# Raw query weights loaded second on SP's queue instead of on ScalarE's, with three dummy matmuls fewer in the ramp

## The chip, the cores and the metric

The kernel runs on one core of a Trainium2 chip. The metric is the device time of one launch in microseconds (us), lower is better. The time before is the median of three runs, 265.23 us (265.18 to 267.19). One more execution is recorded by the hardware profiler; all views of the profile come from that one.

## The reference

One sequence of 2048 tokens of width 448 goes through two blocks with adaptive layer norm. Scale, shift and gate of each come from one conditioning vector `c`. Block A is linear attention with 16 heads of width 28; its features are the softmax of a small product with `w_phi` and the softmax of the negated product. Block B is a gated MLP whose gate mixes tokens with a 2048 x 2048 matrix.

```python
mod = (_silu(c) @ w_mod).reshape(c.shape[0], 6, 1, -1)      # sa, ca, ga, sb, cb, gb
h = _layernorm(x) * (1 + ca) + sa
x = x + ga * A(h, wqkv, w_phi, wo)
#   A: q, k, v = split(h @ wqkv); pq = q @ w_phi; pk = k @ w_phi   (per head)
#      phi_q = [softmax(pq), softmax(-pq)]; phi_k alike
#      o = phi_q @ (phi_k^T v) / (phi_q . sum(phi_k) + 1e-6);  o @ wo
h = _layernorm(x) * (1 + cb) + sb
x = x + gb * B(h, w_in, w_sp, b_sp, w_out)
#   B: z = gelu(h @ w_in); z1, z2 = halves; g = w_sp @ layernorm(z2) + b_sp;  (z1 * g) @ w_out
```

All inputs and the output are in bf16.

## The kernel before, in words

The path that runs is `fast_path`. The tokens are 16 tiles of 128; the width of 448 is cut into four chunks of 112. The kernel is written as many small steps (functions of one or two letters). The text `ORDER` (line 482 on) lists every step with its arguments, and the program emits them in that order, so the order on each engine is this list filtered by engine, written out by hand. In a word such as `FTq:0@B1` the part after the colon is the step's argument and `@B1` is the PSUM slot; in `ld:wk/Y` the letter after the slash is the engine: Y is SP (SyncE), S ScalarE, V VectorE, G GpSimd. Engines wait for one another through semaphores that the framework sets. A DMA's semaphore is one of eight, taken in the order of the loads in the list over all queues; a load that takes a semaphore again waits for the transfer that had it before.

Before the main work the projections are prepared from the raw weights; this is the ramp, the first 17 us:

- `ld:x0` (line 641), `ld:c` (640), `ld:wq` and `ld:wk` (both through `load_rows`, line 630), `ld:phi` (634), `ld:x1`, `ld:x2` (642, 643), `ld:wsa`, `ld:wca` (637), `ld:wv` (630) and further loads are DMAs from HBM. Before, `ld:c` and `ld:wq` are issued by ScalarE, all the other loads of the ramp by SP.
- `du:n` (line 712) issues n matmuls of a zero tile into a PSUM bank that nobody reads; these are the dummies. `du:14@A2` stands directly ahead of the first transposes of the query weights.
- `ct` and `ce:1` to `ce:4` (723 to 736) form silu(c).
- `FTq:h` and `FTk:h` (line 795) transpose half of the raw query or key weights on TensorE, 8 transposes each. `ETq` and `ETk` (799 on ScalarE, 801 on VectorE) copy the results out of PSUM.
- `bd` (739) spreads `phi` into a block-diagonal tile `BD`; `PFq:m` and `PFk:m` (811) multiply the transposed weights with it, 4 products of 112 columns each; `EPq` and `EPk` (799, 801) copy the folded weights out.
- `l1s`, `l1e`, `l1r`, `l1a` (818 to 829) are the layer norm of a tile of x; `X:i` (842) turns a tile of it on TensorE, and `XE:i` (799) copies it out to `hT`.
- `csA` and `ccA` (747) form the shift and scale columns from `wsa` and `wca`; `SHq`, `SHk`, `SHv` (761) and `SC...` (770, 774) put them into the weights.

After the ramp come the products of query, key and value (`qM`, `kM`, `vM`: lines 907, 852, 860), the attention, the second block and the output. Later tiles of the layer norm are turned by DMA transposes on SP's queue (`T1`, line 834).

These few lines show how a load and the dummies are emitted:

```python
def load_rows(eng, dst, src):
    eng.dma_start(out=dst, in_=src.rearrange("(k p) n -> p k n", p=CB))
"wq": lambda q: load_rows(q, wq_raw[0:CB], A_wqkv[:, 0:D]),
def du(n, slot):
    wps = bank(slot, "warm_ps")
    for _ in range(n):
        nc.tensor.matmul(wps[:, 0, 0:256], lhsT=zero[:, 0:P], rhs=zero[:, 0:256], start=True, stop=True)
```

Of the kernel before, what the change touches and what calls it, by code (L numbers as in the profile page):

```python
# [479 lines left out]


ORDER = """
m3 m4 m1/G m2b/V m2a/V ld:x0/Y l1s:0 ld:c/S ld:wq/S du:3@A2 ct@B0 tbl ce:1 ce:2 l1e:0,1/G l1r:0,1 l1a:0/G ce:3 ce:4 du:14@A2 FTq:0@B1 du:1@A2 FTq:1@B0
ETq:0/S X:0@A2 XE:0/S ld:wk/Y FTk:1@A1 ETk:1/S FTk:0@B1 ETk:0/S ld:phi/Y ETq:1/V bd/V scb ld:x1/Y l1s:1 l1e:1,2/G l1r:1,2 l1a:1/G PFq:3@B0 PFq:2@A2
PFq:1@A1 EPq:2/S EPq:1/S ld:x2/Y EPq:3/V l1s:2 l1s:3 l1e:2,4/G l1r:2,4 du:4@A0 PFk:0@B0 PFk:2@B1 PFq:0@A2 PFk:1@A0 ld:wsa/Y du:1@A1 csA@A1 EPk:0/S
EPk:1/S PFk:3@B0 X:1@A0 EPk:3/S XE:1/S EPk:2/S EPq:0/V esA SHq@A2 ld:wca/Y ccA@B0 l1a:3/V X:3@A1 l1a:2/V ecA SCq:0/V SCq:3/V SCq:2/V SCq:1/V X:2@A0
# [692 lines left out]
```

## Time and profile before

| | |
|---|---|
| median of 3 runs | 265.23 us (265.18 to 267.19) |
| the profiled execution: its time, its span | 265.23 us, 263.3 us |
| TensorE matmuls busy | 253.3 us, 96% of the span |
| VectorE, ScalarE, GpSimd busy | 157.6, 107.7, 89.6 us |
| DMA queues q1 (SP's) and q10 (ScalarE's) | 24.05 MB and 0.82 MB |

The span runs from the first to the last instruction; times in the views are counted from its start. PE is TensorE's matmuls, PEld its weight loads, DVE is VectorE, ACT ScalarE, POOL GpSimd; SPq and ACTq are the instruction queues of SyncE and ScalarE that issue DMAs. A timeline row gives the start and the duration of a group of instructions, the operation with its output and inputs, a count, and in square brackets the idle time of the engine ahead of it and what ended it. Instructions on TensorE overlap: a duration runs to the end of the last one in the group, so the spacing of the starts is shorter than the duration of one. In a row of windows stand the stretch, its length, the busy time and count for PE, PEld, DVE, ACT and POOL, the granted clock, the busy share of the DMA engines and their GB/s. The chain of waits is followed back from the last instruction to what released each step.

### The profile page before, as it was taken

The page shows a single profiled execution, that of the slowest core. Times are in us where ns is not written, and L with a number is a line of the kernel's source. Part 1 is how long each engine was busy: PE and PEld are TensorE (multiplying, and loading weights), DVE is VectorE, ACT ScalarE, POOL GpSimd, SP SyncE. Part 2 cuts the span into 40 slices and gives each one's busy share as a digit, 9 for nine tenths or more (in the row PEclk, how much of TensorE's full clock was granted, in tenths as well). Part 3 has the DMA queues.
Part 4 walks back from the last instruction along what each step waited for, and adds up shares of the span by engine and source line. Part 5 has one row for each costly group of instructions (what it writes and reads, how often), then busy time and mean ns, then how long its engine had stood idle before and what let it go on. Part 6 is the DMA issues. An engine that isn't in the chain of part 4 may idle for free.

```text
span 263.3 us, 4375 instructions
## 1 busy us (share of the span) xinstructions
PE 253.3 (96%) x1648; PEld 137.1 (52%) x1648; DVE 157.6 (60%) x367; ACT 107.7 (41%) x222; POOL 89.6 (34%) x149
## 2 busy tenths in 40 slices
PE   6999999999799999999999999999999999999992
PEld 4864565675464554544444444444444444565691
DVE  4689999868799999785106223522371183415761
ACT  2789887646788888987720300100000000000000
POOL 6217986996388888573300000000000000000000
PEclk9999999999999999999999999999999999999999
DMA  7993987993356557869900000002009800030011
GB/s 173 277 294 69 245 149 153 213 288 76 60 96 121 107 107 133 167 131 174 169 0 4 0 0 0 20 2 75 0 2 142 157 0 2 17 105 2 0 37 61
DMA packets 68655, 25.23 MB, mean 96 GB/s; under 512 B 58129, under 2 KB 68498, under 8 KB 68626
## 3 DMA queue, kind: packets, MB, share of 16 engines
q1 hardware_dynamic: 67696, 24.05, 43.8%
q10 hardware_dynamic: 930, 0.82, 1.2%
q8 instruction: 15, 0.25, 0.4%
q14 instruction: 14, 0.11, 0.1%
HBM read 8.87 MB, written 1.84 MB: 41 GB/s over the span
## 4 chain that ended last, share of the span: by engine, by line
PE 90%; DVE 4%; DMA 2%; ACT 1%; issue 1%; POOL 1%; ACTq 0%
PE g_ps L1060 37%; PE z_ps L1044 9%; PE z_ps L1016 9%; PE o_ps L1073 8%; PE q_ps L907 5%; PE v_ps L860 4%; PE k_ps L852 4%; PE x_ps L972 3%; PE kvacc L883 3%; DMA f_wq_raw<-in_A_wqkv_dram 2%; PE num L935 2%; DVE f_t L956 2%; PE tps L795 1%; PE sh_ps L761 1%; PE sh_ps L766 1%
## 5 line engine op out<-in xcount | busy, mean ns | idle before, releaser
L1060 PEld LDWEIGHTS <-f_z2n 128*128 128x128 bf16 x560 | 50.1, 98 | 47.0
L1066 DVE TENSOR_TENSOR f_gb<-g_ps,f_bsp 128x512 f32<-128x512 f32 (+2 forms) x35 | 20.4, 583 | 55.5 <-PE g_ps L1060 55.3
L1060 PE MATMUL g_ps<-f_Eq,f_z2n 128*128 128x512 bf16 x224 | 49.5, 379 | 0.0
L1047 ACT ACTIVATE f_z1T<-z_ps 128x512 bf16<-128x512 f32 x28 | 15.6, 592 | 61.8 <-PE z_ps L1044 61.7
L1016 PE MATMUL z_ps<-f_win,f_hT 112*128 112x448 bf16 (+1 forms) x128 | 26.2, 352 | 0.0
L1044 PE MATMUL z_ps<-f_hT,f_win 113*128 113x512 bf16 (+1 forms) x112 | 26.1, 379 | 0.0
L1060 PE MATMUL g_ps<-f_hT,f_z2n 128*128 128x384 bf16 (+1 forms) x224 | 25.1, 272 | 0.0
L1060 PE MATMUL g_ps<-f_wsp,f_z2n 128*128 128x512 bf16 x112 | 24.7, 379 | 0.0
L1073 PE MATMUL o_ps<-f_wout,f_z1T 128*128 128x448 bf16 x112 | 23.0, 352 | 0.0
L1076 DVE TENSOR_TENSOR f_xpad<-o_ps,f_x 128x448 bf16<-128x448 f32 x16 | 9.6, 620 | 20.7 <-PE o_ps L1073 20.7
L1067 DVE TENSOR_TENSOR f_z1T<-f_gb,f_z1T 128x512 bf16<-128x512 f32 (+2 forms) x35 | 20.5, 585 | 1.8 <-DVE f_gb L1066 0.5
L1016 PEld LDWEIGHTS <-f_hT 112*128 112x128 bf16 (+1 forms) x128 | 12.2, 97 | 12.4 <-DMA f_hT<-f_xpad 0.8
L912 ACT ACTIVATE f_Eq<-q_ps 112x1024 bf16<-112x1024 f32 x16 | 16.1, 1030 | 5.7 <-PE q_ps L907 5.6
L1044 PEld LDWEIGHTS <-f_win 113*128 113x128 bf16 (+1 forms) x112 | 10.9, 97 | 13.0
L855 ACT ACTIVATE f_E<-k_ps 128x448 bf16<-128x448 f32 x32 | 15.9, 550 | 4.1 <-PE k_ps L852 2.5
L866 DVE TENSOR_REDUCE f_ksum<-f_E 128x32 f32<-128x896 bf16 x16 | 16.7, 1060 | 0.7 <-ACT f_E L855 0.7
L956 DVE TENSOR_TENSOR f_t<-num,f_w 128x896 bf16<-128x896 f32 x16 | 16.8, 1084 | 0.0
L1020 ACT ACTIVATE f_z2g<-z_ps 128x896 bf16<-128x896 f32 x16 | 14.7, 916 | 4.0 <-PE z_ps L1016 3.9
L1073 PEld LDWEIGHTS <-f_z1T 128*128 128x128 bf16 x112 | 10.9, 98 | 10.1
L907 PE MATMUL q_ps<-f_hT,f_Wq 113*128 113x512 bf16 (+1 forms) x64 | 15.0, 378 | 0.0
L860 PE MATMUL v_ps<-f_wv,f_hT 113*128 113x448 bf16 (+1 forms) x64 | 14.6, 352 | 0.0
L852 PE MATMUL k_ps<-f_Wk,f_hT 113*128 113x448 bf16 (+1 forms) x64 | 14.5, 352 | 0.0
(165 smaller groups left out, 347.3 us busy)
## 6 DMA issues: line engine op xcount, KB each, us to landing
out_dram<-f_xpad SPq DMA_DIRECT2D x16, 112.0 KB, 1.8
f_win<-in_B_w_in_dram SPq DMA_DIRECT2D x2, 784.0 KB, 5.7
f_x<-in_A_x_dram SPq DMA_DIRECT2D x3, 448.0 KB, 8.6
f_wm<-in_w_mod_dram SPq DMA_DIRECT2D x3, 406.0 KB, 5.7
f_wmg<-in_w_mod_dram SPq DMA_DIRECT2D x2, 392.0 KB, 9.5
f_wout<-in_B_w_out_dram SPq DMA_DIRECT2D x1, 784.0 KB, 6.9
f_bsp<-in_B_b_sp_dram SPq DMA_DIRECT2D x1, 512.0 KB, 4.5
f_wm<-in_w_mod_dram ACTq DMA_DIRECT2D x1, 406.0 KB, 5.0
```

Source lines behind the costliest of these rows:

```text
L852: nc.tensor.matmul(t[:, 0, 0:D], lhsT=hT[0:KR[m], i, m, :], rhs=Wk[0:KR[m], m, :], start=(m == 0), stop=(m == KC - 1))
L860: nc.tensor.matmul(t[:, 0, 0:D], lhsT=hT[0:KR[m], i, m, :], rhs=wv[0:KR[m], m, :], start=(m == 0), stop=(m == KC - 1))
L866: nc.vector.tensor_reduce(out=ksum[:, i], in_=Er[i % NR][:].rearrange("p s (c f h) -> p (s c) h f", c=4, h=HP), axis=AX.X, op=ALU.add)
L907: nc.tensor.matmul(t[:, u, :], lhsT=Wq[0:KR[m], m, cc * CB:cc * CB + P], rhs=hT[0:KR[m], 4 * st:4 * st + 4, m, :], start=(m == 0), stop=(m ...
L912: nc.scalar.activation(out=Eq[st // 2][0:CB, 2 * c2:2 * c2 + 2, s, (st % 2) * 512:(st % 2 + 1) * 512], in_=ps["q" + str(n)][0:CB, :, :], f ...
L956: nc.vector.tensor_tensor(out=tr[i % 2][:], in0=numv(i)[:, :, :, 0:DH], in1=wr[i // 2 % 2][:, i % 2].unsqueeze(3).to_broadcast([P, 2, H, D ...
L1016: nc.tensor.matmul(t[:, hf, 0:D], lhsT=hT[0:KR[m], i, m, :], rhs=win_s[0:KR[m], m, FH + hf * D:FH + (hf + 1) * D], start=(m == 0), stop=(m ...
L1044: nc.tensor.matmul(t[:, 0, :], lhsT=win_s[0:KR[m], m, fc * P:(fc + 1) * P], rhs=hT[0:KR[m], 4 * st:4 * st + 4, m, :], start=(m == 0), stop ...
L1060: nc.tensor.matmul(g[:, 0, 0:b - a], lhsT=later["z2n"][:, s_, fc * P:(fc + 1) * P], rhs=wspT[t][:, s_, a:b], start=(s_ == 0), stop=(s_ == ...
L1066: nc.vector.tensor_tensor(out=gb, in0=ps["G%d_%d" % (ch, fc)][:, 0, 0:b - a], in1=bsp[:, t * TCHF + a:t * TCHF + b], op=ALU.add)
L1067: nc.vector.tensor_tensor(out=z, in0=gb, in1=z, op=ALU.mult)
L1073: nc.tensor.matmul(ps["o" + str(t)][:, 0, 0:D], lhsT=later["z1T"][:, fc, t * P:(t + 1) * P], rhs=wout_s[:, fc, :], start=(fc == 0), stop=( ...
```

## The change

`ld:wq` keeps its place in the list but goes from ScalarE's queue (`/S`) to SP's (`/Y`), where it comes directly after `ld:x0` and ahead of `ld:wk`. `du:14` becomes `du:11`. On SP's queue every later load and transpose stands one place further back; on ScalarE's queue the load of `c` is directly followed by the table load. TensorE has three weight loads and three matmuls fewer. Nothing else is changed: the semaphores that the loads take are the same, as the order of the list is.

```diff
 ORDER = """
-m3 m4 m1/G m2b/V m2a/V ld:x0/Y l1s:0 ld:c/S ld:wq/S du:3@A2 ct@B0 tbl ce:1 ce:2 l1e:0,1/G l1r:0,1 l1a:0/G ce:3 ce:4 du:14@A2 FTq:0@B1 du:1@A2 FTq:1@B0
+m3 m4 m1/G m2b/V m2a/V ld:x0/Y l1s:0 ld:c/S ld:wq/Y du:3@A2 ct@B0 tbl ce:1 ce:2 l1e:0,1/G l1r:0,1 l1a:0/G ce:3 ce:4 du:11@A2 FTq:0@B1 du:1@A2 FTq:1@B0
 ETq:0/S X:0@A2 XE:0/S ld:wk/Y FTk:1@A1 ETk:1/S FTk:0@B1 ETk:0/S ld:phi/Y ETq:1/V bd/V scb ld:x1/Y l1s:1 l1e:1,2/G l1r:1,2 l1a:1/G PFq:3@B0 PFq:2@A2
 PFq:1@A1 EPq:2/S EPq:1/S ld:x2/Y EPq:3/V l1s:2 l1s:3 l1e:2,4/G l1r:2,4 du:4@A0 PFk:0@B0 PFk:2@B1 PFq:0@A2 PFk:1@A0 ld:wsa/Y du:1@A1 csA@A1 EPk:0/S
 EPk:1/S PFk:3@B0 X:1@A0 EPk:3/S XE:1/S EPk:2/S EPq:0/V esA SHq@A2 ld:wca/Y ccA@B0 l1a:3/V X:3@A1 l1a:2/V ecA SCq:0/V SCq:3/V SCq:2/V SCq:1/V X:2@A0
```

## The prediction

> **What bounds the kernel now.** I read the page's totals first, then the chain of waits for the first 20 us, then the timelines of TensorE, SP's queue and ScalarE there, and last the waits further on.
>
> ```profile
> span 263.3 us, 4375 instructions
> PE 253.3 (96%) x1648; PEld 137.1 (52%) x1648; DVE 157.6 (60%) x367; ACT 107.7 (41%) x222; POOL 89.6 (34%) x149
> PE 90%; DVE 4%; DMA 2%; ACT 1%; issue 1%; POOL 1%; ACTq 0%
> ```
>
> TensorE is busy for 96% of the span and is 90% of the chain that ends last. DMA is 2% of that chain, and the chain's first 20 us show that this is the load of the raw query weights, 5.47 of 263.3 us (start, duration, what):
>
> ```profile
> 0.72 0.54 ACTq L640
> ...
> 1.29 5.47 DMA f_wq_raw<-in_A_wqkv_dram
> ...
> 6.80 0.99 PE tps L795 x8
> ...
> 8.01 0.75 PE tps L795 x8
> ...
> 9.97 0.92 ACT f_wTk L799
> ```
>
> Up to 6.76 us the end of the kernel hangs on that one transfer: ScalarE's queue issues it second, at 1.29, and it lands 5.47 us later. TensorE's timeline shows what surrounds it:
>
> ```profile
> 2.51 3.17 PE L712 MATMUL warm_ps<-f_zero 128*128 128x256 bf16 x14
> 6.80 0.99 PE L795 MATMUL tps<-f_ident,f_wq_raw 112*112 112x112 bf16 x8 [1.13 <-DMA f_wq_raw<-in_A_wqkv_dram]
> 7.59 0.42 PE L712 MATMUL warm_ps<-f_zero 128*128 128x256 bf16 x1
> 8.98 1.45 PE L795 MATMUL tps<-f_ident,f_wk_raw 112*112 112x112 bf16 x16
> 11.13 0.60 PE L712 MATMUL warm_ps<-f_zero 128*128 128x256 bf16 x4
> 12.40 0.37 PE L811 MATMUL pf_ps<-f_BD,f_wTk 112*112 112x112 bf16 x4
> ...
> 16.91 1.90 PE L907 MATMUL q_ps<-f_hT,f_Wq 113*128 113x512 bf16 x8
> ```
>
> The fourteen dummies end at 5.68; then TensorE idles 1.13 us. A dummy comes every (3.17 - 0.42) / 13 = 0.21 us in the first row and about every 0.11 us at 11.13 (0.60 us for four, with an end of some 0.27): TensorE runs at half speed at first. (The column of the granted clock below says 1.00 even there; the spacing is the better witness.) The tile view of the key weights puts the change of speed inside their sixteen transposes, between 9 and 10 us (min/median/max in ns):
>
> ```profile
> L795 PE MATMUL tps<-f_ident,f_wk_raw x16: 215/300/301, 9.0 to 10.2; 112*112 112x112 bf16 x16
> ```
>
> So the fast clock came some 3.1 us after unbroken work began at 6.80, and it had not come by the end of the 3.17 us of dummies.
>
> **The change, part by part.** SP's queue and the landings (KB are 1024 bytes; the last column is us from issue to landing):
>
> ```profile
> 0.72 0.39 SPq L641 DMA_DIRECT2D f_x<-in_A_x_dram  x1
> 1.18 0.41 SPq L630 DMA_DIRECT2D f_wk_raw<-in_A_wqkv_dram  x1
> 1.64 0.48 SPq L634 DMA_DIRECT2D f_phi<-in_A_w_phi_dram  x1
> ...
> 6.78 0.39 SPq L644 DMA_DIRECT2D f_x<-in_A_x_dram  x1
> ```
> ```profile
> f_wk_raw<-in_A_wqkv_dram SPq DMA_DIRECT2D x1, 392.0 KB, 4.9
> f_wq_raw<-in_A_wqkv_dram ACTq DMA_DIRECT2D x1, 392.0 KB, 5.5
> f_phi<-in_A_w_phi_dram SPq DMA_DIRECT2D x1, 24.5 KB, 5.4
> ```
>
> *The load.* Its issue goes to 1.18, the present place of the key weights: 0.11 us earlier. What counts is what it shares the engines with. Now the two weights are in flight together and land at 6.76 (query) and 6.08 (key). In one queue the query weights come first and the key weights wait behind them. The traffic of these microseconds prices that (window, the busy columns, PEclk, DMA share, GB/s):
>
> ```profile
> 1.50:2.50 1.00, 1.00 (x7) 0.51 (x5) 0.93 (x5) 0.83 (x1) 1.00 (x7) 1.00 0.65 141
> 2.50:3.50 1.00, 1.00 (x6) 0.73 (x6) 0.96 (x6) 0.72 (x3) 0.31 (x1) 1.00 0.68 164
> 3.50:4.50 1.00, 1.00 (x7) 0.70 (x5) 0.71 (x5) 0.00 (x0) 0.46 (x3) 1.00 1.09 345
> 4.50:5.50 1.00, 1.00 (x6) 0.51 (x4) 0.00 (x0) 0.00 (x0) 0.89 (x3) 1.00 1.14 254
> 5.50:6.50 1.00, 0.18 (x1) 0.00 (x0) 0.00 (x0) 0.00 (x0) 0.94 (x2) 1.00 1.23 212
> 12.90:22.40 9.50, 9.47 (x88) 5.59 (x88) 8.29 (x26) 8.84 (x17) 2.59 (x6) 1.00 0.91 237
> ```
>
> x0 is 115 kB (128 x 448 x 2), each weight 401 kB. Moved in sum: 141 kB by 2.5, 305 by 3.5, 650 by 4.5, 904 by 5.5. Both weights, x0, c and phi (943 kB) are through at about 5.68; the query weights landed at 6.76, 1.1 us later. x0 plus the query weights are 516 kB, which this traffic reaches at 3.5 + 211/345 = 4.11; with the same 1.1 us the landing is **5.2**. The bounds: not before 4.84, where the shortened dummies end (below), and not after 6.08, where the key weights landed from this very place with a rival beside them. I take 5.2, as the first full-rate window (345) belongs to this stretch. That one queue can fill the engines is seen in the last row: from 12.90 on, with all loads on SP's queue, they are 91% busy.
>
> *What is behind it on SP.* All later issues slip by one issue, 0.41 us. The key weights: the same bytes ahead, so by 5.57 + 1.1 = 6.7; their first transposes stood at 8.98, or 6.9 to 7.2 after the shift, and ScalarE can't take their result before 7.9 (below), so 0.5 us is to spare. phi lands at 7.0 now and, with the same bytes ahead, then too; its user on VectorE (next row) would start at about 7.6. SP's issue at 6.78 waits for the query weights' landing (it reuses their semaphore) and comes earlier, not later; the engines are full anyway. All this is costed at nothing; without the cover each would cost its lateness, a few tenths.
>
> ```profile
> 9.34 0.61 DVE L739 TENSOR_TENSOR f_BD<-f_phi,f_bmask 112x448 bf16<-112x448 bf16 x1
> ```
>
> *ScalarE* loses one issue of 0.35 us before its table load; it is idle afterwards for 4.61 us (first row below), so nothing comes of it.
>
> *The dummies.* Eleven end at 2.51 + 11 x 0.2115 = 4.84 instead of fourteen at 5.47 (issue). They stand in front of the transposes in TensorE's order: with fourteen, a landing at 5.2 would be used only at 5.47, so this edit is worth 0.27 us of the sum.
>
> *The start of the transposes* therefore moves from 6.80 to about 5.2: **-1.6 us** (ends -0.7 and -1.96). What is late next? ScalarE's timeline:
>
> ```profile
> 7.84 0.91 ACT L799 COPY f_wTq<-tps 112x896 bf16<-112x896 bf16 x1 [4.61 <-PE tps L795]
> 9.22 0.59 ACT L799 COPY f_hT<-xt_ps 128x512 bf16<-128x512 bf16 x1 [0.48 <-PE xt_ps L842]
> 9.97 1.71 ACT L799 COPY f_wTk<-tps 112x896 bf16<-112x896 bf16 x2 [0.16 <-PE tps L795]
> 11.57 0.98 ACT L799 CAST f_Wq<-pf_ps 112x448 bf16<-112x448 f32 x2
> 13.76 0.53 ACT L799 CAST f_Wk<-pf_ps 112x448 bf16<-112x448 f32 x1 [0.34 <-PE pf_ps L811]
> ```
>
> From 7.84 on it is almost full, and waits 0.48 + 0.16 = 0.64 us for slow transposes. This is where the clock enters. The idle stretch shrinks from 1.13 us to about 0.4, so TensorE's work is nearly unbroken from 2.51 on; if 3.1 to 3.2 us of that bring the fast clock, it comes between 5.7 and, counted from the landing, 8.4, instead of near 9.9. A transpose then costs some 52 ns instead of 94: 0.75 us for eight in the chain's row at 8.01 against (0.37 - 0.215) / 3 for the fast products of the same width at 12.40. The two waits go. I estimate **-0.5 us** of the possible 0.64; the ends are 0 and, with the 0.34 at 13.76 too, -0.98. VectorE, which has no such waits before 13.5 but for its first, sets a limit of about 2 on the whole shift. Its normalised tiles (first row, done at 14.82) feed the transposes of the chain's row at 15.09, with 0.3 us of slack:
>
> ```profile
> 14.12 0.70 DVE L829 TENSOR_SCALAR f_xpad<-f_x,f_nm,f_rs 128x448 bf16<-128x448 bf16 x2 [0.43 <-POOL f_rs L826]
> ```
> ```profile
> 15.09 0.47 PE xt_ps L842 x8
> ```
>
> Here a rule of the Trainium skill ("TensorE: Matmul & The Clock Gate", Part 1) bears: the clock doubles after one busy window of about 3.4 us, and the windows run freely, so work of one window's length may straddle two. The trace agrees so far: 3.17 us of dummies didn't suffice. By the rule alone the term is the full 0.64 at a good phase, and 0 at a bad one.
>
> *From there to the end* TensorE is the bound and the shift is carried: 9.47 of 9.50 us busy from 12.90 to 22.40, and between 17 and 80 us its own waits are
>
> ```profile
> PE num L940 <- DVE f_t L956: 1.8, 1, 1.8
> PE kvacc L883 <- POOL f_phik L873: 0.4, 1, 0.4
> ```
>
> both on engines whose work descends from the same ramp and so moves with it. The sum is -1.6 - 0.5 = **-2.1 us**. The profiled execution took 265.23 us, its span 263.3 and 1.9 around it; that is also the median shown, so I forecast **263.1 us**.
>
> **The rivals.** *Earlier start, same clock* (-1.1 to -1.6): the fast clock comes near 9.9 again, and the twelve or so 112-wide products that ran fast after 9.9 run slow, at 42 ns more each 0.5 us, partly hidden. For it speaks that 3.17 us of dummies failed; against it that the gap shrinks. About 263.9.
>
> *The transfer hardly arrives earlier.* The window 2.50 to 3.50 moved only 164 GB/s; if that is the price of one queue starting, the query weights land as the key weights do, at 6.08: -0.7, 264.5. The Trainium skill ("DMA: Bandwidth & Descriptors", Issuing engines are not separate DMA queues) goes further: the issuing engine changes only issue time, as all queues share the engines. Read so, only the 0.11 us of issue is won, 265.1. Against it stands that the order of the bytes, not their rate, is changed.
>
> *Slower: the clock is lost.* If the landing stays near 6.1 while the dummies end at 4.84, the gap is 1.25 us instead of 1.13; should that delay the fast clock by another 3.2 us, to 13, then 32 products (42 ns each, 1.3 us), five dummies (0.1 each, 0.5) and 16 column products are slow, some 2.0 us less 0.5 of waits that hide it: +1.5 - 0.7 = +0.8, 266.0. It decides only from a landing past about 6.0.
>
> *More than forecast:* start at 4.84 and all of the 0.98: -2.9, 262.3.
>
> **How the numbers follow.** Forecast 0.60 (262.6 to 263.6); same clock 0.16; late landing 0.10; clock lost, or anything slower, 0.06; more 0.08. The prediction is the likeliest case's. The range 262.4 to 264.5 takes it, the same clock and most of the late landing. About 1% (2.65 us) is what a measurement here can tell from no change: below 262.6 lie the last case and the edge of the first, 0.12; above 267.9 next to nothing, 0.03; between, 0.85.
>
> **What would show it.** The query weights landing near 5.2 with about 4 us from issue; transposes of them starting there with an idle of under 0.5 us before; durations of 215 ns already in the key weights' first transposes; ScalarE's 0.48 and 0.16 gone; the first query product, at 16.91 now, near 14.8. A landing past 5.8, 300 ns throughout the key weights, or a wait of theirs on their DMA, would make it wrong; so would a first query product that is early while the span is not shorter.

## The result, and the profile after

| | before | changed |
|---|---|---|
| median of 20 runs each | 265.27 us (263.49 to 267.35) | 263.84 us (262.72 to 266.19) |
| ratio of the means of these runs, with its 95% interval | | 0.9936 (0.991 to 0.9963) |
| the profiled execution: time, span | 265.23 us, 263.3 us | 263.9 us, 262.0 us |
| means of all runs, later ones included (116 and 32) | 265.23 us | 264.13 us |
| ratio of these means, with its 95% interval | | 0.9959 (0.9944 to 0.9974) |

The change saves 1.4 us by the medians and 1.7 by the means of the first 20 runs each, and 1.1 us (0.7 to 1.5) by the means of all. Single runs of either kernel lie up to 4 us apart, and the comparison of 20 with 20 runs isn't sharp: the kernel before, compared with itself, came out at 0.9961 (0.9922 to 0.9999) of itself. The means over all runs rest on the most of them, and why the runs differ so much turned out to be part of the answer. One run of the kernel with the key weights first (268.53 us) is over 1.5% above its fastest and is left out below, and one like it of the kernel before (267.59 us) moves no difference by more than 0.03 us.

TensorE's timeline of the changed kernel, the rows that answer to those shown before:

```profile
2.49 2.53 PE L712 MATMUL warm_ps<-f_zero 128*128 128x256 bf16 x11
4.89 1.00 PE L795 MATMUL tps<-f_ident,f_wq_raw 112*112 112x112 bf16 x8
5.67 0.42 PE L712 MATMUL warm_ps<-f_zero 128*128 128x256 bf16 x1
...
7.06 1.30 PE L795 MATMUL tps<-f_ident,f_wk_raw 112*112 112x112 bf16 x16
...
9.14 0.60 PE L712 MATMUL warm_ps<-f_zero 128*128 128x256 bf16 x4
...
14.93 1.90 PE L907 MATMUL q_ps<-f_hT,f_Wq 113*128 113x512 bf16 x8
```

The idle 1.13 us ahead of the first transposes is gone, they start at 4.89 instead of 6.80, and the first query product at 14.93 instead of 16.91. SP's queue and the landings:

```profile
1.17 0.42 SPq L630 DMA_DIRECT2D f_wq_raw<-in_A_wqkv_dram  x1
1.64 0.48 SPq L630 DMA_DIRECT2D f_wk_raw<-in_A_wqkv_dram  x1
2.17 0.49 SPq L634 DMA_DIRECT2D f_phi<-in_A_w_phi_dram  x1
...
5.42 0.58 SPq L644 DMA_DIRECT2D f_x<-in_A_x_dram  x1
```
```profile
f_wq_raw<-in_A_wqkv_dram SPq DMA_DIRECT2D x1, 392.0 KB, 3.7
f_wk_raw<-in_A_wqkv_dram SPq DMA_DIRECT2D x1, 392.0 KB, 4.6
...
f_phi<-in_A_w_phi_dram SPq DMA_DIRECT2D x1, 24.5 KB, 4.3
```

The query weights land 3.7 us after their issue instead of 5.5, at 4.84; the key weights at 6.26 and phi at 6.5, both ahead of their users. Of the traffic up to this landing (GB/s in the last column) only the stretch from 2.5 to 3.5 us changed much, from 164 to 218; the next has 342 where it had 345:

```profile
2.50:3.50 1.00, 1.00 (x6) 0.72 (x6) 0.95 (x6) 0.34 (x3) 0.31 (x1) 1.00 0.77 218
3.50:4.50 1.00, 1.00 (x7) 0.72 (x5) 0.71 (x5) 0.00 (x0) 0.47 (x3) 1.00 1.09 342
```

ScalarE still waits 0.48 us for the transposes of x; the 0.16 further on is gone:

```profile
5.92 0.91 ACT L799 COPY f_wTq<-tps 112x896 bf16<-112x896 bf16 x1 [3.07 <-PE tps L795]
7.30 0.59 ACT L799 COPY f_hT<-xt_ps 128x512 bf16<-128x512 bf16 x1 [0.48 <-PE xt_ps L842]
7.99 1.71 ACT L799 COPY f_wTk<-tps 112x896 bf16<-112x896 bf16 x2
11.78 0.53 ACT L799 CAST f_Wk<-pf_ps 112x448 bf16<-112x448 f32 x1 [0.34 <-PE pf_ps L811]
```

Set side by side, instruction by instruction, TensorE in the profile of the changed kernel is 1.92 us early at the first transposes, 1.98 at the first query product, 1.85 from 40 us on, and 1.46 from 114 us on. The last 0.4 us went to a wait that the kernel before did not have in its profile, for a DMA transpose (waits of TensorE):

```profile
PE z_ps L1016 <- DMA f_hT<-f_xpad: 0.3, 1, 0.3
```

In a second profile of the same kernel (below) this wait is 0.2 us, and 2.0 us are carried to the end.

### The profile page after: what moved, and what is told of

Same layout as the page of the kernel before. It is cut to its first block, busy times and chain, and to the rows that moved or that the text cites. A ratio compares the mean times of both kernels' runs of the same rounds, so it can differ in the third digit from the quotient of the medians.

```text
span 262.0 us, 4360 instructions
## 1 busy us (share of the span) xinstructions
PE 252.3 (96%) x1636; PEld 136.5 (52%) x1645; DVE 157.7 (60%) x367; ACT 107.7 (41%) x222; POOL 89.5 (34%) x149
## 4 chain that ended last, share of the span: by engine, by line
PE 90%; DVE 4%; DMA 1%; issue 1%; ACT 1%; POOL 1%; SPq 0%
PE g_ps L1060 37%; PE z_ps L1044 9%; PE o_ps L1073 8%; PE z_ps L1016 8%; PE q_ps L907 5%; PE v_ps L860 4%; PE k_ps L852 4%; PE x_ps L972 3%; PE kvacc L883 3%; PE num L935 2%; DVE f_t L956 2%; PE warm_ps L712 2%; DMA f_hT<-f_xpad 1%; PE tps L795 1%; PE sh_ps L761 1%
```

## The experiments

Three theories stood against each other for where the gain is from. (The recorded expectations letter their own theories anew each time.) A: the order of the bytes; the query weights' bytes now come ahead of the key weights', and that start is carried to the end. B: the queue itself, SP's being quicker than ScalarE's. C: the clock, that is, how unbroken TensorE's work is while it waits. Differences of means stand with 95% intervals; the mean of the kernel before is 265.23 (116 runs), that of the changed kernel 264.13 (32). "Clock" is the mean granted clock of a run. The trace also records when the fast clock was granted; ahead of the first record the column of a view reads 1.00, so that it doesn't show the half speed at the start. The edits show only those words of `ORDER` that differ.

**The kernel before, again.** No edit.

> The kernel before once more, for its spread and the granted clock of each run. The twenty runs of the changed kernel lie in two groups: clock 0.997 to 0.999 with 262.7 to 263.9 us, and 0.990 to 0.993 with 264.25 to 266.2. Theory A: the groups come from the fast clock being lost for one stretch later in the kernel in some runs, and have nothing to do with the change: then the kernel before shows the same two groups, some 1.5 to 2 us apart, in about the same shares (the lower clock in 3 to 6 of 10), and the median of its 0.997 to 0.999 runs is about 1.5 to 2 above that of the changed kernel's, 264.9 to 265.3. Theory B: the change caused the lower group: then the kernel before has no clocks under 0.997.

Twelve runs: seven with a clock of 0.998 to 1.000 (263.5 to 264.9 us), five with 0.990 to 0.992 (264.85 to 266.55). Where each run's clock is known, 49 of 96 runs of the kernel before have a clock of 0.993 or less, with a mean of 266.10 against 264.13; of the changed kernel 12 of 32, 264.96 against 263.64. So the two groups are not of the change's making. But the expectation missed the distance of the upper groups: the changed kernel's is 0.49 us faster (0.12 to 0.82), not 1.5 to 2; in the lower groups it is 1.14 (0.67 to 1.57). The windows of this run's profile show what the lower group is:

```profile
63.80:67.10 3.30, 1.52 (x9) 0.69 (x8) 3.08 (x7) 2.91 (x6) 0.98 (x1) 1.00 0.44 89
67.20:70.50 3.30, 3.30 (x30) 2.41 (x29) 1.25 (x6) 0.94 (x4) 0.95 (x1) 0.50 0.37 70
70.70:74.00 3.30, 3.30 (x29) 1.97 (x28) 2.78 (x4) 2.87 (x6) 2.07 (x5) 1.00 0.03 5
```

In the first stretch TensorE is busy for 1.52 of 3.30 us; in the next the clock granted is 0.50. The idle time is one wait, in front of the nine dummies of `dm:9,3`:

```profile
64.39 0.92 PE L766 MATMUL sh_ps<-f_win,f_Gb 112*128 112x448 bf16 x4
67.09 0.40 PE L940 MATMUL num<-f_zero 128*128 128x32 bf16 x9 [1.78 <-DVE f_t L956]
67.33 1.76 PE L935 MATMUL num<-f_KVbd,f_Eq 112*128 112x120 bf16 x16
```

After it, sixteen products take 1.76 us; at full clock they take 1.00. The records of all traces lie on a grid of 3.413 us (in this one the clock came at 5.73, went at 67.17 and was back at 70.59), and where the grid stands to the start of the kernel differs from run to run. That is the phase, and it decides whether the 1.78 us fall into one stretch of the grid (clock lost in five of the six profiles of this study that have all of the wait, or all but 0.02 us, in one stretch) or are cut in two (kept, in the two profiles shown first). An estimate: a phase that is equally likely everywhere would put 1.78 us whole into one stretch of 3.41 in (3.41 - 1.78) / 3.41 = 48% of the runs, and 49 of 96 is 51%.

**The load alone.** Changed kernel with fourteen dummies:

```diff
-ce:3 ce:4 du:11@A2 FTq:0@B1
+ce:3 ce:4 du:14@A2 FTq:0@B1
```

> The load goes to SP's queue, the fourteen dummies stay. Theory A (the order of the bytes decides, and the dummies stand in the way): the query weights land at 4.9 as in the changed kernel, but the transposes start behind the dummies, at 5.5 instead of 4.89; the first query product at about 15.5 (14.93 in the changed kernel, 16.91 before); time 0.6 us above the changed kernel, ratio to before 0.995 to 0.997. Theory B (the dummies hide behind the landing): start at 4.9 and the same time as the changed kernel.

Landing at 5.08, start behind the dummies at 5.46, as theory A of the expectation has it. But the first query product came at 14.53, earlier than in any profile of the changed kernel, and the mean of twelve runs is 263.82: 0.31 us below the changed kernel (-0.88 to +0.24), not 0.6 above it. The tile view of the query weights tells why; the median transpose is a fast one (min/median/max in ns):

```profile
L795 PE MATMUL tps<-f_ident,f_wq_raw x16: 213/215/301, 5.5 to 6.5; 112*112 112x112 bf16 x16
```

The clock came at 5.87, right after a stretch of the grid (2.46 to 5.87) filled by dummies. ScalarE's 0.48 us of waiting is gone there:

```profile
6.26 0.91 ACT L799 COPY f_wTq<-tps 112x896 bf16<-112x896 bf16 x1 [3.41 <-PE tps L795]
7.07 0.59 ACT L799 COPY f_hT<-xt_ps 128x512 bf16<-128x512 bf16 x1
7.54 1.73 ACT L799 COPY f_wTk<-tps 112x896 bf16<-112x896 bf16 x2
```

**The dummies alone.** The load back on ScalarE's queue, eleven dummies:

```diff
-ld:c/S ld:wq/Y
+ld:c/S ld:wq/S
```

> Eleven dummies, the load stays on ScalarE's queue. Theory A: the load lands at 6.76 as before, the idle time ahead of the transposes grows from 1.13 to about 1.75 us, the first query product stays at 16.9 if the fast clock comes in the same way: ratio 1.000. Theory B (the dummies are what the gain is made of): start earlier than 6.8, ratio 0.995. Theory C (a longer idle stretch costs the fast clock): the fast clock comes later than 3.4 us after the first transpose, the first query product at 17.5 or later, ratio above 1.002.

Landing at 6.76, idle 1.79 us, clock at 11.25, first query product at 17.04. Mean 265.70: 0.47 above the kernel before (-0.23 to +1.14). Theory B of the expectation, that the gain is made of the dummies, is out; whether the longer idle time costs anything can't be told from this (eight of the twelve runs have a clock of 0.993 or less, more than the half of before).

**The key weights first.** Both on SP's queue, in the other order:

```diff
-ld:c/S ld:wq/Y du:3@A2
+ld:c/S ld:wk/Y ld:wq/Y du:3@A2
-XE:0/S ld:wk/Y FTk:1@A1
+XE:0/S FTk:1@A1
```

> Both weights on SP's queue, the key weights ahead of the query weights, eleven dummies. Theory A (the gain is that the query weights' bytes are no longer interleaved with another load's and come first): now the key weights land at about 4.9 and the query weights at about 6.2, where the key weights land in the changed kernel; the transposes start at 6.2 to 6.8, the first query product at 16.3 to 16.9, ratio 0.998 to 1.000. Theory B (SP's queue is faster than ScalarE's, whatever the order): query weights land by 5.4 and most of the gain stays, ratio 0.994 to 0.996.

```profile
f_wk_raw<-in_A_wqkv_dram SPq DMA_DIRECT2D x1, 392.0 KB, 4.1
f_wq_raw<-in_A_wqkv_dram SPq DMA_DIRECT2D x1, 392.0 KB, 4.9
```

The key weights land at 5.3, the query weights, on the same queue, at 6.58. The place in the queue decides, not the queue: theory A. The mean of eleven runs, 265.98, is even 0.78 above the kernel before (+0.15 to +1.40); beside the 35 runs of before in the same comparison the ratio is 1.0031 (0.999 to 1.0071). With eleven dummies and a late landing TensorE idles 1.71 us, and in the profile the clock, granted at 4.69, was taken away from 8.10 to 11.51. That this is the 0.78 us isn't shown: the first query product of this profile came at 16.41, and the profiles of before have 15.63 to 16.91.

**Both on ScalarE's queue.** Query, then key weights behind c; SP's queue goes on with phi and x:

```diff
-ld:c/S ld:wq/Y du:3@A2
+ld:c/S ld:wq/S ld:wk/S du:3@A2
-XE:0/S ld:wk/Y FTk:1@A1
+XE:0/S FTk:1@A1
```

> Query and key weights both on ScalarE's queue, in this order, behind c; SP's queue goes on with phi, x1 and so on right after x0. Eleven dummies. Theory A (what counts is that no other queue has bytes in flight beside the query weights): x0, phi, x1, x2 and the modulation weights share the engines with them, and they land at 5.6 to 6.5; the first query product at 15.7 to 16.6; mean 0.7 to 1.3 above the changed kernel's. Theory B (only the order of the two weights counts): they land by 5.2 and the mean is that of the changed kernel, 264.0.

```profile
f_wq_raw<-in_A_wqkv_dram ACTq DMA_DIRECT2D x1, 392.0 KB, 4.5
f_wk_raw<-in_A_wqkv_dram ACTq DMA_DIRECT2D x1, 392.0 KB, 6.3
```

Landing at 5.80, between the 4.84 to 5.55 of the kernels with the load second on SP's queue and the 6.7 of before: being first in one queue helps only as far as the other queue has little in flight. Theory A by the landing; it is one profile, and how much SP's queue had in flight was not varied further. The first query product came at 16.0. The mean, 265.88, missed the expectation: it is 1.75 above the changed kernel, not 0.7 to 1.3, and 0.66 above before (+0.10 to +1.20) although the weights land earlier. Eight of the twelve runs have a clock of 0.993 or less; what the rest of the difference is made of isn't shown.

**Few dummies.** Changed kernel with four:

```diff
-ce:3 ce:4 du:11@A2 FTq:0@B1
+ce:3 ce:4 du:4@A2 FTq:0@B1
```

> The changed kernel with four dummies instead of eleven ahead of the first transposes: TensorE idles from 3.4 to 4.9 us. Theory A (the landing sets the start, the dummies only keep the work unbroken for the clock): start at 4.9 as in the changed kernel; the fast clock comes one stretch of 3.4 us later in about half of the phases, so the first query product at 14.9 to 16.0 and the mean 0.3 to 0.8 us above the changed kernel's. Theory B (the dummies ahead do nothing): the same mean as the changed kernel's 264.0.

```profile
5.60 0.62 PE L795 MATMUL tps<-f_ident,f_wq_raw 112*112 112x112 bf16 x4 [2.08 <-DMA f_wq_raw<-in_A_wqkv_dram]
```

Here the landing was at 5.55, the clock came at 10.82, and the first query product at 16.18. The mean of 265.49 is 1.36 above the changed kernel (+0.83 to +1.88): the whole gain is lost. The dummies ahead of the landing are worth as much as the load's new place, which fits theory C and is more than either the prediction or this expectation had. That the clock carries the whole of it rests on this one profile.

**The changed kernel, again.** No edit.

> The changed kernel once more, beside the same runs of the kernel before, for the size of the difference: the query weights land near 4.9, the transposes start at 4.9, mean 263.7 to 264.3, ratio of the means to the kernel before 0.993 to 0.997. If the first comparison was luck of the phases, the ratio is 0.998 or more.

Mean of twelve 264.39; ratio of this comparison 0.9974 (0.994 to 1.0009), a little beyond the upper end of what was expected. Its profile has the phase of the first profile of before (3.18 against 3.16), and there the change shows in full: landing at 5.44 (4.9 expected), start at 5.49, clock at 6.59 (9.99 before), first query product at 14.90, TensorE 2.0 us early at its end. All transposes of the key weights are fast, and ScalarE no longer waits its 0.48 and 0.16 us:

```profile
L795 PE MATMUL tps<-f_ident,f_wk_raw x16: 213/215/215, 7.2 to 8.0; 112*112 112x112 bf16 x16
```
```profile
7.38 0.58 ACT L799 COPY f_hT<-xt_ps 128x512 bf16<-128x512 bf16 x1
7.86 1.72 ACT L799 COPY f_wTk<-tps 112x896 bf16<-112x896 bf16 x2
```

So the start is 1.32 us earlier in this pair of profiles and the first query product 2.01: here the clock gives 0.69 us.

**Without `dm:9,3`.** The dummies that stand in front of products 4 and 5 near 66 us, and wait for VectorE, are taken out of the changed kernel:

```diff
-SHw:1@B1 dm:9,3 nM:4@A1
+SHw:1@B1 nM:4@A1
```

> The changed kernel without the nine dummies of dm:9,3, which wait for VectorE near 66 us and hold up the products behind them. Theory A (the lower group of the granted clock, 0.990 to 0.993, comes from this idle stretch of 1.78 us: where one of the clock's stretches of 3.41 us holds all of it, the next one runs at half speed): without them the idle stretch is some 0.4 us, all runs have clocks of 0.997 or more, the upper half of the times (264.25 to 266.2 in the changed kernel) is gone, and the products start about 1 us earlier: 261.5 to 263.2. Theory B (the clock is lost elsewhere): the two groups stay, only shifted.

> The changed kernel without dm:9,3 once more beside the three others of this call: mean 261.8 to 262.6, clocks 0.997 or more in nearly all runs, no run above 263.5.

Six runs with a mean of 262.18 and eight with 262.10, 2.00 us below the changed kernel (-2.44 to -1.56). The wait of 1.78 us becomes one of 0.41 for ScalarE (the second of these profiles):

```profile
64.46 0.92 PE L766 MATMUL sh_ps<-f_win,f_Gb 112*128 112x448 bf16 x4
65.79 1.00 PE L935 MATMUL num<-f_KVbd,f_Eq 112*128 112x120 bf16 x16 [0.41 <-ACT f_Eq L912]
```

No run of the fourteen has a clock of 0.993 or less, where 12 of 32 had; in neither profile is the clock lost near 66 us. Four runs lie under the expected 0.997, at 0.995 and 0.996. One of them is profiled, and there the clock falls only at 258.19, when TensorE's last product has ended at 255.99. So theory A holds for the place, and the lower group of the clock is gone, as is the direct wait of some 1.4 us.

**The same for the other three kernels**, so that the change can be seen without this loss: the kernel before, the load alone, and the kernel before with nineteen dummies (`du:19` in place of `du:14`), all without `dm:9,3`.

> The kernel before without dm:9,3, so that the clock loss near 66 us no longer hides the size of the change. Theory A (the change is worth what its earlier start gives, some 1.1 to 1.7 us on average over the phases): mean 263.2 to 263.9, against 262.2 for the changed kernel without dm:9,3. Theory B (the change is worth something only through where the clock is lost later): mean 262.0 to 262.6.

> The load on SP's queue, fourteen dummies, no dm:9,3. Theory A (the three dummies are in the way of a landing at 4.8 to 5.5): start at 5.5, mean 0.2 to 0.5 above the changed kernel without dm:9,3. Theory C (what the dummies cost at the start they return by an unbroken stretch for the clock, as the landing spreads from 4.8 to 5.5): the same mean or up to 0.3 below.

> The load stays on ScalarE's queue (landing at 6.7) and nineteen dummies fill the time up to about 6.5; no dm:9,3. This is the clock alone: work is unbroken from 2.5 us on, and the start of the transposes stays at 6.7 to 6.8. Theory A (the earlier landing is the main part, the clock worth 0.3 to 0.6 us): mean 0.3 to 0.6 under the kernel before without dm:9,3, and 0.7 to 1.2 above the changed one; the first query product at 16.2 to 16.6. Theory B (an unbroken stretch is all that counts): as fast as the changed kernel without dm:9,3.

| without `dm:9,3` | runs | mean us | against before without it |
|---|---|---|---|
| before: load on ScalarE, 14 dummies | 12 | 262.63 | |
| changed: load on SP, 11 dummies | 14 | 262.13 | -0.50 (-1.04 to +0.01) |
| load on SP, 14 dummies | 6 | 261.71 | -0.92 (-1.47 to -0.41) |
| load on ScalarE, 19 dummies | 7 | 262.23 | -0.40 (-0.88 to +0.04) |

The change is worth 0.5 us here, just at the edge of what these runs can tell, and not the 1.1 to 1.7 of theory A; the mean of before, 262.63, lies at the upper end of what theory B gave. The twelve runs of before are eight from 261.7 to 262.5 and four from 263.4 to 264.0, while no run of the changed kernel is above 262.8: the change takes away the slow third rather than moving every run. (Which phase those four had isn't recorded.) Fourteen dummies are better than eleven by 0.42 (0.00 to 0.82), the direction that theory C named, though more than it had. And dummies that merely fill the time to the old landing do as much as the change (0.09 apart, -0.23 to +0.43), which is theory B of that expectation; their first query product was expected at 16.2 to 16.6 and came at 15.84. The load alone without `dm:9,3` beats both kernels of the case: ratio 0.989 (0.985 to 0.993) to the kernel before beside it.

The profiles show what happened. The kernel before, at a phase of 2.09, has its fast clock at 5.50, ahead of the transposes; the changed kernel, at a phase of 2.19, has none until 9.02 (the tile view of the query weights, first before, then changed, both without `dm:9,3`):

```profile
L795 PE MATMUL tps<-f_ident,f_wq_raw x16: 212/215/257, 7.0 to 8.0; 112*112 112x112 bf16 x16
```
```profile
L795 PE MATMUL tps<-f_ident,f_wq_raw x16: 300/300/342, 5.3 to 7.0; 112*112 112x112 bf16 x16
```

The profiles of these four ramps, each kernel's in order of phase (the first point of the grid after the start, us; "no dm" is without `dm:9,3`):

| kernel | phase | landing | first transpose | fast clock at | first query product |
|---|---|---|---|---|---|
| before, no dm | 2.09 | 6.98 | 7.02 | 5.50 | 15.95 |
| before, again | 2.32 | 6.66 | 6.70 | 5.73 | 15.63 |
| before | 3.16 | 6.76 | 6.80 | 9.99 | 16.91 |
| changed | 0.91 | 4.84 | 4.89 | 7.74 | 14.93 |
| changed, no dm | 2.05 | 5.19 | 5.23 | 8.88 | 15.34 |
| changed, no dm, again | 2.19 | 5.29 | 5.33 | 9.02 | 15.44 |
| changed, again | 3.18 | 5.44 | 5.49 | 6.59 | 14.90 |
| load alone, no dm | 0.83 | 5.24 | 5.47 | 7.66 | 15.26 |
| load alone | 2.46 | 5.08 | 5.46 | 5.87 | 14.53 |
| before with 19 dummies, no dm | 0.28 | 6.73 | 6.78 | 7.11 | 15.84 |

At a phase near 3.2 the change is worth 2.0 us, near 2.1 to 2.3 only 0.2 to 0.6: there fourteen dummies fill a whole stretch of the grid and have the clock up before the weights land, and eleven, with a gap of 0.20 and 0.32 us before the landing, do not. A gap alone doesn't decide it: at the phase of 3.18 the changed kernel has one of 0.47 us, and the clock came at the end of that stretch.

## Why the prediction was right, and where it was not

The direction and the range hold (263.84 in 262.4 to 264.5); the saving was forecast at 2.1 us and is 1.4 by the medians, 1.1 by the means of all runs. By its number the result is that of the rival *Earlier start, same clock* (263.9), but not by its mechanism: the clock did not come near 9.9 again, it came between 6.59 and 9.02 in the four profiles of the changed kernel. That the first pair of profiles shows 1.98 us at the first query product, so near the 2.1, is luck: 0.3 us more at the start than forecast, 0.44 less from the clock, and two different phases.

*The load.* Right. The landing was put at 5.2; seven profiles with the load second on SP's queue have 4.84, 5.08, 5.19, 5.24, 5.29, 5.44 and 5.55, a mean of 5.23. The order of bytes as the cause stands on two experiments (key weights first, both on ScalarE's queue). The rival of a late landing is out. The Trainium skill ("DMA: Bandwidth & Descriptors", Issuing engines are not separate DMA queues) says that using several issuing engines saves only issue time. The runs agree that the queue as such is worth nothing (6.58 on SP's queue behind the key weights), but by that sentence alone the gain would have been missed, as what moved was the order.

*What is behind it on SP.* Right: the key weights at 6.26 to 7.02 in these profiles (6.7 forecast), phi at 6.5 in the first of them, nobody waiting for either there.

*The start of the transposes.* Right in size: -1.6 forecast, -1.92 and -1.32 in the two profiles of the changed kernel against the first of before.

*The dummies.* Not borne out. Taking out three was to be worth 0.27 us, since they stand before the landing. They do, in the profile with the landing at 4.84, and near that phase the first query product comes 0.33 us later with fourteen (15.26 against 14.93, with a later landing, too); but the landing spreads up to 5.55, and the fourteen also hold the clock's stretch. Both pairs of kernels put eleven behind fourteen, by 0.31 (-0.24 to +0.88) and by 0.42 (0.00 to 0.82). Neither interval holds a gain of 0.27; that fourteen are better is likely, not shown.

*The clock.* This is the term that was off: "I estimate -0.5 us of the possible 0.64". At the phase that the prediction read, near 3.2, it came out: 0.69 us, with the fast key weights and without ScalarE's two waits. In the first profile of the changed kernel it gave 0.06 (1.92 at the start, 1.98 at the first query product), the transposes of the key weights were fast only from about the middle (215/224/301 ns), and the 0.48 us stayed. The estimate took the one profile of before, whose phase is the bad one, for the kernel, and counted 3.1 to 3.2 us from the start of unbroken work, where the records show fixed points of a grid. At other phases the kernel before has the fast clock before its transposes (5.50 and 5.73), and then the change takes it away instead of bringing it (8.88 and 9.02). This is the rival *Slower: the clock is lost*, at landings of 5.19 and 5.29, where the prediction let it decide only from past 6.0; the earlier start outweighs it there. The page of the Trainium skill that was named ("TensorE: Matmul & The Clock Gate", Part 1) says that the windows run freely. The traces agree, on a grid of 3.413 us, and the prediction should have followed that into the kernel before, too. Over the profiles of the table the transposes start 1.6 us earlier (6.84 to 5.24 in the mean of three and four), and the first query product comes 1.0 earlier (16.16 to 15.15): counted over these phases, the clock's term is a loss of 0.6 us.

*From there to the end.* Carried, but not without loss in each run: 1.98 became 1.46 in one profile, 2.0 stayed 2.0 in the other. Not seen at all was the loss of the clock near 66 us, which hits 49 of 96 runs of before and 12 of 32 of the changed kernel; the runs hit are slower by 2.0 us in the one and by 1.3 in the other. Among the runs not hit the change is worth 0.49 us, as much as without `dm:9,3`. Whether the loss really hits the changed kernel less often, and so makes up the difference to 1.1 us, stays open: 38% of 32 runs is not clear of the 48% that one phase as likely as another would give.

## What to carry to other kernels

Where the first work waits for one transfer, look at what else is in flight when it lands: putting its bytes ahead of a rival's in one queue brought it 1.5 us forward with little more traffic. Filler matmuls before a landing are not only a delay to be cut to the landing time; here they also kept the work unbroken for the clock (four instead of eleven cost 1.36 us), and cutting them to the earliest landing leaves a gap in all the later ones. Before a clock's effect is read from one profile, profile the same kernel a few times: its runs may differ more than the kernels do.

## What the runs showed of the hardware

The granted clock changes only on a grid of 3.413 us, whose phase to the kernel's start differs from run to run. A stretch filled by dense matmuls brought the fast clock at its end (idle time up to 0.07 us in it, e.g. from 2.32 to 5.73); stretches with 0.8 us idle or more at the start did not. Between, 0.23 and 0.47 us idle brought it, and 0.21, 0.22, 0.31, 0.32 and 0.40 did not. These five stretches also held two to four of the one-row transposes of c, but one that held all four and no idle time brought it (1.27 to 4.69), so what decides there stays open.

Once fast, stretches with 1.17 to 1.39 us idle kept the clock. Five of the six profiles that held the wait of 1.78 us near 66 us in one stretch lost it for the next 3.41 us, and so did a stretch of the ramp with 1.71 us idle (4.69 to 8.10, key weights first); the sixth (stretch 66.13 to 69.54, 1.77 us) and one with 1.69 us of the wait in a stretch kept it. The runs with such a loss are 1.3 us (changed kernel) to 2.0 us (before) slower; 3.41 us at half speed can be at most 1.7 of that (an estimate), and the phase that brings the loss sets the clock of the ramp, too.

Dummies that wait for another engine themselves didn't help against it: `dm:9,3` stood behind the wait that it should have filled, and without it the changed kernel is 2.0 us faster, some 1.4 of them by the shorter wait (1.78 to 0.41 us).
